# Left sums of the twice-split output projection dealt behind its second and third results, the second sequence's norm scaled three blocks per step, and the third sequence's first gate loads ahead of weight sums

## The chip, the cores and the metric

One core of one Trainium2 chip. The metric is the device time in microseconds of one execution, as the median of three runs; a profiled execution of the same kernel gives the instruction times below. The engines of the core work side by side and wait for each other through semaphores: TensorE (PE, matmuls; its weight loads, PEld, overlap them), VectorE (DVE), ScalarE (ACT), GpSimd (POOL) and SyncE (SP), which issues nearly all the DMA transfers of this kernel.

## The reference

All inputs are float32. Attention over 8 sequences of 12 heads, 448 tokens and 64 values, then a gated feed-forward layer on the result:

```python
q_n, k_n = rmsnorm(q, g_q), rmsnorm(k, g_k)
scores = (1 / sqrt(64)) * q_n @ k_n.T        # per sequence and head, 448 x 448
attn = softmax(scores)
o = attn @ v
x = o as (8*448, 12*64)                      # 3584 tokens, 768 values
xn = x / sqrt(mean(x*x) + 1e-6) * rms_g
g = xn @ w_gate                              # 768 x 1536
h = g * sigmoid(g) * (xn @ w_val)            # 768 x 1536
out = h @ w_out                              # 1536 x 768
```

## The kernel before

**Tiling and order.** Two heads make a pair; 6 pairs make a sequence, and the 48 pairs run in one long loop. A block of the loop computes the scores of pair g in seven steps (`step`, L659 for scores) and, in the same steps, the weighted values of pair g-1 (L674), with an exp on ScalarE for each step (L664). Between blocks `fill` deals out the matmuls of the feed-forward layer. While the attention of sequence b runs, the layer's gate and value products of sequence b-1 and the output projection of sequence b-2 are dealt out. Sequences are counted from 0 in the code (b = 1 is the second). Every piece of PE work goes through `pe`, which advances a counter `now["t"]` by one; `after(n, fn)` has `fn` recorded n pieces later. Each engine works through its own instructions in the order in which they were recorded, so the place in which a helper is called sets what stands ahead of what.

**Fewer multiplications.** Most products are done by schemes that trade multiplications for additions. Gate and value (`three`, L1178) use 15 products instead of 18 for a split of the tokens' matrix by 2 and 3 and of the weights by 3 and 3; the left sums for it are L772, the right sums L1083 and L1086 (`derive`), and the results are added up by DVE in L1196 and L1199. Output projection has two forms: `out_strassen` (L1443) for the second and the fifth sequence, and `out_quads` (L1514) for the third, fourth, sixth, seventh and eighth, where a 2 x 2 split with seven products is nested twice. The first sequence is multiplied plainly (L1582, L1316), and while that goes on the weights are brought in and converted (`convert`: ScalarE L907 and L908, DVE L913 to L915, POOL L964) and stored to device memory in `kept`, `kept_q` and `kept_o`, from where they are loaded again for each sequence.

**A quad.** `out_quads` runs seven outer products i = 0 to 6, in the order of `ORDER_Q`; each is one "quad" of seven inner products, and 11 blocks of weights of up to 192 KB (kind `wq`) are loaded for it. PE gets them in four pieces: `a(i)` multiplies A11 and A12, `bb(i)` multiplies S2 and S3, `c(i)` multiplies A22 and S1, and `d(i)` multiplies S4 and adds into the second half of `c`'s bank. The order on PE is a(i+1), d(i), bb(i+1), c(i+1), a(i+2), and so on. A piece of two products is six matmuls, `d` is three; each matmul stands as two records in the profile. The results are read by DVE: L1534 after `a` (with a ScalarE copy, L1533), L1539 and L1540 after `bb`, L1552 after `c`, L1557 after `d`. L1552 reads the whole bank of `c`, so `d(i)` may write it only when L1552 has ended.

The left sums S1 to S4 (`left_q1`, L1388) are additions of 128 x 384 blocks on DVE:

```python
(("S1", "A21", "A22", ALU.add), ("S2", "S1", "A11", ALU.subtract),
 ("S3", "A11", "A21", ALU.subtract), ("S4", "A12", "S2", ALU.subtract))
```

S1, S2 and S4 go to tiles of `l2_pool`, which has 5; S3 overwrites A21. `bb(i)` records, behind L1540, S4 of quad i and S1, S2 and S3 of quad i+1; they stand on DVE ahead of L1552 of `c(i)`. For i = 1 the rest of the outer left sums (L1360, in `first_sums`) is recorded between them by `hurry`. `"l2 done"` is noted at i = 5; from there on two of the next sequence's L772 sums may take tiles of the same pool.

**Norm.** `norm_x(b)` spreads the reciprocal root of each token over 128 partitions by a matmul into a bank `rb` (L738) of the four banks that scores use, and then multiplies each of x's six blocks by it (`scale`, L744, DVE). For b = 0 all six are recorded at once, for the others one per piece of PE work.

**Loads and their room.** Blocks of weights share one arena with a planner of free pieces (`places`, `room`, `block`). `uses` lists all loads in the order in which they will be needed; `ask` issues the next of them (L1062) when room is left for `keep_free` + 1 blocks, and it is called whenever a block has been used up. `derive_q` makes the sums of w_out's inner split for the quads, once: 21 sets, each with two loads (`wx`, L1044), two blocks of room, four DVE subtractions (L1146 to L1149) and four stores (L1153, L1156). `derive_o` makes those of the outer split (L1118): 24 subtractions. Both are called in `fill` after each piece of PE work.

Of the kernel before, what the change touches and what calls it, by code (L numbers as in the profile page):

```python
# [335 lines left out]
def safe_scores(  # L336
# [37 lines left out]
    st = {}  # L374


    now, due = {"t": 0}, []

    def after(n, fn):
        due.append((now["t"] + n, fn))  # L380
# [351 lines left out]
    def norm_x(b):  # L732


        rs = st.pop(("rx", b))
        ps = (ps_s if b else ps_f).tile([128, 512], F32, name="rb", tag="s" if b else "f")
        for t in range(NT):
            nc.tensor.transpose(ps[:, t * P:(t + 1) * P], rs[:, t:t + 1].to_broadcast([P, 128]), ident[0:P, 0:P])  # L738

        whole = st["x", b]  # L740

        def scale(hp):
            x = whole[:, hp, :]
            nc.vector.scalar_tensor_tensor(x, x, rg[:, hp:hp + 1], ps[:, 0:S], ALU.mult, ALU.mult)  # L744

        for hp in range(NPAIR):
            if b:
                after(hp, lambda hp=hp: scale(hp))
            else:
                scale(hp)  # L750
        if b == 0:
            return

        parts = st.pop(("x", b)).rearrange("p (h c) n -> p h c n", h=2)
        a = st["left", b] = {f"a{i + 1}{k + 1}": parts[:, :, k, i * HT:(i + 1) * HT] for i in range(2) for k in range(3)}

        def place(name):
            if name in OVER:
                return a[OVER[name]]
            if name in MADE[:4]:  # L760
                t = s_pool.tile([128, S], F32, name="xs")
            elif name in ("S2", "S0"):
                t = l2_pool.tile([128, S], F32, name="l2")
            else:
                t = more_x[("S4", "S5", "S13").index(name)]
            return t.rearrange("p (h n) -> p h n", h=2)

        def op(name):
            first, second, what = LEFT_G[name]
            one, two = a[first], a[second]  # L770
            a[name] = place(name)
            nc.vector.tensor_tensor(a[name], one, two, what)  # L772

        slow.extend((name, lambda name=name: op(name)) for name in MADE)
        st["x_at"] = now["t"]
# [98 lines left out]
    def room(many, kind="w"):  # L874
        return len(places(kind)) >= many
# [140 lines left out]
    for b in range(1, B):  # L1016
# [5 lines left out]
        else:  # L1022
            for name in ORDER_O:
                for c in range(NFP):
                    uses.append(("wo", b, name, c))
    asked = {"n": 0, "derived": 0}
    side = [("wd", 1, half, fp) for fp in range(NFP) for half in BLOCKS]
    side += [("wx", 2, ORDER_Q[i], c) for i, j in jobs_q for c in (j, j + KG)]
    derived = [(g, to) for g in GROUPS for _, _, to in PRODUCTS if to in RIGHT_G]
# [6 lines left out]
    def ask():  # L1036

        if turn_of["n"] < TURNS:
            return
        while side and (room(1, "side") or side[0][0] == "wd" and asked["derived"] > 32 and room(4, "wg")):  # L1040
            key = side.pop(0)
            asked[key] = now["t"]
            st[key] = block("side" if room(1, "side") else "wg")
            nc.sync.dma_start(out=data(key), in_=home(key))  # L1044
        while asked["n"] < len(uses):
            key = uses[asked["n"]]
            kind, keep_free = "wg" if key[0] == "wg" else "w", 3
            if key[1] == 1 and key[0] == "wg":
                kind, keep_free = "wg1", 6
            elif asked["derived"] < len(derived):  # L1050
                return
            if key[0] == "wo" and key[2][0] == "T" and ("kept", *key[2:]) not in asked:
                return
            if key[0] == "wq" and asked.get("sums_q", 0) < KG * (key[2] + 1):
                return
            if not room(keep_free + 1, kind):
                return
            asked["n"] += 1
            asked[key] = now["t"]
            st[key] = block(kind)  # L1060
            src = home(key)
            nc.sync.dma_start(out=data(key)[:, 0:src.shape[-1]], in_=src)  # L1062
# [67 lines left out]

    def derive_q(wait=5):

        if not todo_q or sums_o or now["t"] - asked.get("at_q", 0) < 3 or not room(2, "wg"):
            return False
        i, j = todo_q[0]
        keys = [("wx", 2, ORDER_Q[i], c) for c in (j, j + KG)]
        for key in keys:
            if asked.get(key, now["t"]) > now["t"] - wait:
                return False
        todo_q.pop(0)  # L1140
        own_a, own_b = ("ta", i, j), ("tb", i, j)
        st[own_a], st[own_b] = block("wg"), block("wg")
        asked["at_q"] = now["t"]
        x, y, ta, tb = (data(key).rearrange("p (h n) -> p h n", h=2) for key in (*keys, own_a, own_b))

        nc.vector.tensor_tensor(tb[:, 1], x[:, 1], x[:, 0], ALU.subtract)  # L1146
        nc.vector.tensor_tensor(ta[:, 1], y[:, 1], x[:, 1], ALU.subtract)
        nc.vector.tensor_tensor(ta[:, 0], y[:, 1], tb[:, 1], ALU.subtract)
        nc.vector.tensor_tensor(tb[:, 0], y[:, 0], ta[:, 0], ALU.subtract)  # L1149

        def store():
            parts = kept_q[i].rearrange("p (n w) -> p n w", w=HW)
            nc.sync.dma_start(out=parts[:, j], in_=x[:, 0])  # L1153
            for src, first, second in ((y, 1, 6), (ta, 2, 3), (tb, 4, 5)):
                gap = (second - first) * KG
                nc.sync.dma_start(out=parts[:, first * KG + j:second * KG + j + 1:gap], in_=src)  # L1156
            asked["sums_q"] = asked.get("sums_q", 0) + 1

        after(1, store)
        for key in (*keys, own_a, own_b):  # L1160
            after(3, lambda key=key: used(key))
        return True
# [295 lines left out]
    def out_quads(b):  # L1458
# [77 lines left out]
        def bb(i):  # L1536
            ps = two(i, "b")
            u = st["u", b, i] = tmp.tile([128, S], F32, name="th", tag="th", bufs=2)[:, 0:BW].rearrange("p (h n) -> p h n", h=2)
            nc.vector.tensor_tensor(u[:, 0], ps[:, 0], st.pop(("q1", b, i)), ALU.add)  # L1539
            nc.vector.tensor_tensor(u[:, 1], ps[:, 1], u[:, 0], ALU.add)  # L1540
            left_q1(b, i, (3,))
            if i == 1:
                hurry(first_sums)
            if i + 1 < len(ORDER_Q):
                left_q1(b, i + 1, range(3))
            if i + 2 == len(ORDER_Q):
                st["l2 done", b] = True

        def c(i):
            ps = two(i, "c")  # L1550
            u3 = st["u", b, i][:, 1:2].to_broadcast([128, 2, HW])
            nc.vector.tensor_tensor(dst[i][1].rearrange("p (h n) -> p h n", h=2), ps, u3, ALU.add)  # L1552

        def d(i):
            ps = bank[i, "c"]
# [67 lines left out]
    def fill(n=None):  # L1623

        if n is None:
            part["slot"] += 1
            upto = part["all"] * min(part["slot"] / part["slots"], 1.0)
            n = 0
            while n < len(todo) and part["spent"] + todo[n][0] / 2 < upto:
                part["spent"] += todo[n][0]  # L1630
                n += 1
        for _ in range(min(n, len(todo))):
            _, turns, sums_made, fn = todo.pop(0)
            while turn_of["n"] < turns:
                if not convert():
                    pe(idle)
            made, key = sums_made or (0, None)
            while asked["derived"] < made or (key and key not in st):
                before = dict(asked)
                derive(0)  # L1640
                if key and key[0] == "wo":
                    derive_o(0)
                ask()
                if before == asked:
                    pe(idle)
            pe(fn)
            convert()

            if first_sums:
                first_sums.pop(0)()  # L1650
            elif slow and now["t"] - st["block"] > 4 and now["t"] - st["x_at"] >= NPAIR and may_make(slow[0][0]):
                slow.pop(0)[1]()
            if 2 < now["t"] - st["block"] < 5:
                derive()
            if now["t"] - st["block"] > 4 and now["t"] != st.get("left_sums"):
                made = 0
                while made < 2:
                    done = derive()
                    if not done:
                        break  # L1660
                    made += done
                for _ in range(0 if made else 3 if asked["derived"] > 32 else 2):
                    derive_o()
                derive_q()

# [239 lines left out]
```

## Time and profile before

| | |
|---|---|
| median of three runs | 1566.55 us (1565.58 to 1568.97) |
| the profiled execution | 1563.31 us |
| its span, first to last instruction | 1561.5 us |
| PE busy, share of the span | 1491.8 us, 96% |
| PEld | 1160.1 us, 74% |
| DVE | 1027.2 us, 66% |
| ACT | 603.8 us, 39% |
| POOL | 734.1 us, 47% |
| mean DMA rate | 207 GB/s |
| mean granted PE clock | 0.990 |

How to read it: PE is busy nearly all the time, so what counts is where it isn't. In the lines below, a row of waits reads "who waited <- for whom: us in total, times, longest us". A row of the time line reads "start us, duration us, engine, line of the kernel, operation, out<-in, size, count", and in brackets the idle time before it with what ended it. A row of stretches reads "from:to, length", then busy time and count for PE, PEld, DVE, ACT and POOL, then the granted share of PE's clock, the share of the time that the DMA engines were busy, and GB/s. Some places in time: the second sequence's norm is at 243 to 259 us, its output projection at 433 to 503, the third's gate products at 507 to 631, and the third's quads at 632 to 704; the other quads lie at 821 to 892, 1171 to 1243, 1359 to 1413 and 1502 to 1553.

### The profile page before, as it was taken

The numbers are of one execution on the slowest core, as the hardware profiler recorded it, in microseconds if no ns is written. First come the engines' busy times: TensorE is split into PE (matmuls) and PEld (weight loads), VectorE is DVE, ScalarE is ACT, GpSimd is POOL, SyncE is SP. The second block draws the span as 40 slices with busy tenths as digits, with TensorE's granted clock in tenths as the row PEclk, the third lists the DMA queues.
The fourth block names the chain that finished last, engine by engine and source line by source line (L and its number), as shares of the span: only waits on it lengthen the run. The fifth ranks groups of instructions, "written<-read, shape, count | busy, mean of one in ns | idle before, by whom it ended". The sixth has DMA issues, their size and how long they took to land.

```text
span 1561.5 us, 25665 instructions
## 1 busy us (share of the span) xinstructions
PE 1491.8 (96%) x8732; PEld 1160.1 (74%) x8732; DVE 1027.2 (66%) x1826; ACT 603.8 (39%) x1377; POOL 734.1 (47%) x708
## 2 busy tenths in 40 slices
PE   8999998998898999999999999999999999999997
PEld 4344444677754888778888789858788789889997
DVE  5787897787855577864568645645668644674664
ACT  6856764343322443224442353434542342201110
POOL 6877986546433353463544545346544533021002
PEclk9999999999999999999999999999999999999999
DMA  7758584675577999976557855576457745488675
GB/s 191 231 152 249 160 253 142 216 246 193 185 229 230 295 302 286 300 235 186 160 151 234 240 169 168 161 227 194 132 159 241 217 139 145 149 270 248 177 216 183
DMA packets 302175, 322.50 MB, mean 207 GB/s; under 512 B 81620, under 2 KB 243668, under 8 KB 302036
## 3 DMA queue, kind: packets, MB, share of 16 engines
q1 hardware_dynamic: 301108, 320.58, 67.3%
q8 instruction: 72, 1.18, 0.3%
q14 instruction: 67, 0.55, 0.1%
q10 hardware_dynamic: 800, 0.20, 0.1%
q0 software_dynamic: 128, 0.00, 0.0%
HBM read 266.90 MB, written 53.77 MB: 205 GB/s over the span
## 4 chain that ended last, share of the span: by engine, by line
PE 79%; DVE 14%; DMA 3%; issue 2%; SPq 1%; ACT 1%; POOL 0%; DVEq 0%; POOLq 0%; ACTq 0%
PE ff L1178 35%; PE ff L1514 12%; PE sc L659 7%; PE av L674 7%; PE ff L1443 5%; PE ff L1582 5%; PE tr L545 2%; PE ff L1316 2%; DVE l L1388 1%; PE den L692 1%; PE den L607 1%; PE sc L563 1%; PE av L590 1%; DVE w L1118 1%; DVE ms L496 1%
## 5 line engine op out<-in xcount | busy, mean ns | idle before, releaser
L714 POOL TENSOR_TENSOR es<-es,e 128x448 f32<-128x448 f32 x205 | 251.0, 1224 | 13.6
L1178 PE MATMUL ff<-x,w 128*128 128x224 f32 x1272 | 254.0, 353 | 1.4 <-DVE pb L1199 1.1
L1178 PEld LDWEIGHTS ff<-x,w 128*128 128x128 f32 x1272 | 238.6, 190 | 4.2 <-DVE pb L1199 1.4
L659 PE MATMUL sc<-qT,kT 64*64 64x448 f32 x1176 | 234.3, 544 | 6.9 <-DVE x L744 5.5
L674 PE MATMUL av<-e,vt 64*64 64x448 f32 x984 | 195.5, 543 | 0.0
L664 ACT ACTIVATE e<-sc 128x448 f32<-128x448 f32 x294 | 154.9, 546 | 83.6 <-PE sc L659 65.5
L1178 PE MATMUL ff<-xs,w 128*128 128x224 f32 x848 | 170.2, 356 | 7.6 <-DMA w<-kept 5.4
L1178 PEld LDWEIGHTS ff<-xs,w 128*128 128x128 f32 x848 | 159.6, 191 | 12.2 <-DVE x L772 4.7
L644 POOL TENSOR_TENSOR ss<-ss,rd 128x448 f32<-128x448 f32 x40 | 46.7, 1168 | 215.3 <-ACT rd L643 215.3
L709 POOL TENSOR_TENSOR es<-e 128x448 f32<-128x448 f32 x41 | 47.2, 1151 | 213.6 <-ACT e L664 213.6
L659 PEld LDWEIGHTS sc<-qT,kT 64*64 64x64 f32 x1176 | 79.7, 134 | 90.8 <-issue 68.2
L1514 PE MATMUL ff<-w,l 128*128 128x192 f32 x630 | 121.4, 337 | 24.5 <-DVE pa L1552 11.2
L1514 PEld LDWEIGHTS ff<-w,l 128*128 128x128 f32 x630 | 106.1, 194 | 32.6 <-DVE pa L1552 12.8
L1199 DVE TENSOR_TENSOR pc<-ff,l 128x448 f32<-128x448 f32 x56 | 34.9, 623 | 134.4 <-PE ff L1178 77.0
L515 POOL TENSOR_TENSOR rs<-ms,mhalf 128x12 f32<-128x12 f32 (+1 forms) x50 | 115.5, 2311 | 4.2
L1582 PE MATMUL ff<-x,w 128*128 128x448 f32 x288 | 111.8, 541 | 0.0
L674 PEld LDWEIGHTS av<-e,vt 64*64 64x64 f32 x984 | 66.7, 134 | 41.4 <-issue 41.4
L1196 DVE TENSOR_TENSOR pb<-ff,pb 128x448 f32<-128x448 f32 x84 | 52.3, 623 | 65.3 <-PE ff L1178 55.9
L1582 PEld LDWEIGHTS ff<-x,w 128*128 128x128 f32 x288 | 53.3, 190 | 51.0 <-issue 47.6
L1178 PE MATMUL ff<-top_x,w 128*128 128x224 f32 x424 | 87.8, 357 | 2.8 <-DVE w L1086 2.8
L1178 PEld LDWEIGHTS ff<-top_x,w 128*128 128x128 f32 x424 | 78.8, 190 | 13.9 <-issue 13.7
L1178 PE MATMUL ff<-l,w 128*128 128x224 f32 x432 | 86.8, 353 | 0.7 <-DVE pc L1199 0.7
(210 smaller groups left out, 2799.1 us busy)
## 6 DMA issues: line engine op xcount, KB each, us to landing
w<-kept SPq DMA_DIRECT2D x383, 256.0 KB, 3.4
w<-kept_q SPq DMA_DIRECT2D x350, 192.0 KB, 3.7
w<-kept_o SPq DMA_DIRECT2D x150, 192.0 KB, 3.7
kept_q<-w SPq DMA_DIRECT2D x63, 192.0 KB, 3.8
qk<-in_q_dram SPq DMA_DIRECT2D x48, 192.0 KB, 3.7
qk<-in_k_dram SPq DMA_DIRECT2D x96, 96.0 KB, 3.7
raw<-in_moe_w_gate_dram SPq DMA_DIRECT2D x24, 384.0 KB, 4.6
raw<-in_moe_w_val_dram SPq DMA_DIRECT2D x24, 384.0 KB, 4.1
```

The lines of the kernel that those rows point to most:

```text
L515: nc.gpsimd.tensor_tensor(st["rs", g][:, cols], ms, mhalf[:, cols], ALU.pow)
L644: after(m, lambda: (nc.gpsimd.tensor_tensor(ss, ss, rd, ALU.add), st.update({("summed", b): hp})))
L659: nc.tensor.matmul(ps[r, 0:S], lhsT=st["kT", g][r, keys_of(i)], rhs=st["qT", g][r, :], start=True, stop=True)
L664: nc.scalar.activation(e, ps[:, 0:S], ACT.Exp)
L674: nc.tensor.matmul(st["av", g][own(j), 0:S], lhsT=vt, rhs=st["e", g, i][r], start=i == 0, stop=i == PARTS - 1, skip_group_check=True)
L709: nc.gpsimd.tensor_tensor(st["es", g], st["e", g, 0], st["e", g, 1], ALU.add)
L714: nc.gpsimd.tensor_tensor(st["es", g], st["es", g], st["e", g, i], ALU.add)
L1178: nc.tensor.matmul(bank[:, w * HT:(w + 1) * HT], lhsT=data(key)[:, (2 * w + c) * 128:(2 * w + c + 1) * 128], rhs=a[left][:, c, :], start=o ...
L1196: nc.vector.tensor_tensor(T[name], ps[:, 0:S], T[name], ALU.add)
L1443: nc.tensor.matmul(ps, lhsT=left_o(b, which, LEFT_O[name], c), rhs=data(("wo", b, name, c)), start=first and c == 0, stop=c == NFP - 1, sk ...
L1514: nc.tensor.matmul(ps, lhsT=a[:, j, :], rhs=data(key)[:, n % 2 * HW:(n % 2 + 1) * HW], start=start and j == 0, stop=j == KG - 1, skip_grou ...
L1582: nc.tensor.matmul(bank[w][:, 0:S], lhsT=data(key)[:, c * 128:(c + 1) * 128], rhs=st["x", 0][:, 3 * half + c, :], start=half == c == 0, st ...
```

## The change

Three things are moved; nothing is added to or taken from the arithmetic.

- In `out_quads`, `bb(i)` now records only S1 of quad i+1. S4 of quad i and S2 and S3 of quad i+1 are recorded in `c(i)`, behind L1552. For i = 1, `hurry` and then S1 of quad 2 stand behind L1552 too. `"l2 done"` is noted in `c`.
- In `norm_x`, blocks 0 to 2 of the second sequence are scaled at once and blocks 3 to 5 one piece of PE work later.
- Seven loads, the first gate weights of the third sequence, are issued when two blocks are free instead of four, and while they are the next to be issued `derive_q` makes no set. `fill` calls `derive_o` twice per piece of work where it called it three times once `derived` was over 32.

```diff
         for hp in range(NPAIR):
             if b:
-                after(hp, lambda hp=hp: scale(hp))
+                after(hp // 3 if b == 1 else hp, lambda hp=hp: scale(hp))
...
+    next_gate = uses.index(("wg", 2, GROUPS[0], PRODUCTS[0][2]))
+    next_gate = range(next_gate, next_gate + 7)
...
             elif asked["derived"] < len(derived):
                 return
+            elif asked["n"] in next_gate:
+                keep_free = 1
...
-        if not todo_q or sums_o or now["t"] - asked.get("at_q", 0) < 3 or not room(2, "wg"):
+        if not todo_q or sums_o or now["t"] - asked.get("at_q", 0) < 3 or asked["n"] in next_gate or not room(2, "wg"):
             return False
...
             nc.vector.tensor_tensor(u[:, 1], ps[:, 1], u[:, 0], ALU.add)
-            left_q1(b, i, (3,))
-            if i == 1:
-                hurry(first_sums)
-            if i + 1 < len(ORDER_Q):
-                left_q1(b, i + 1, range(3))
-            if i + 2 == len(ORDER_Q):
-                st["l2 done", b] = True
+            if i == 0 or i > 1 and i + 1 < len(ORDER_Q):
+                left_q1(b, i + 1, (0,))
 
         def c(i):
             ps = two(i, "c")
             u3 = st["u", b, i][:, 1:2].to_broadcast([128, 2, HW])
             nc.vector.tensor_tensor(dst[i][1].rearrange("p (h n) -> p h n", h=2), ps, u3, ALU.add)
+            left_q1(b, i, (3,))
+            if i == 1:
+                hurry(first_sums)
+                left_q1(b, i + 1, (0,))
+            if i + 1 < len(ORDER_Q):
+                left_q1(b, i + 1, (1, 2))
+            if i + 2 == len(ORDER_Q):
+                st["l2 done", b] = True
...
-                for _ in range(0 if made else 3 if asked["derived"] > 32 else 2):
+                for _ in range(0 if made else 2):
                     derive_o()
                 derive_q()
```

## The prediction

> **What bounds it now.** First the page's shares: TensorE (PE) is busy for nearly the whole span, no other engine comes near.
>
> ```profile
> span 1561.5 us, 25665 instructions
> PE 1491.8 (96%) x8732; PEld 1160.1 (74%) x8732; DVE 1027.2 (66%) x1826; ACT 603.8 (39%) x1377; POOL 734.1 (47%) x708
> ```
>
> So a gain must come out of PE's idle time or of its clock. Second, PE's waits (total, times, longest): that short list is what there is to win.
>
> ```profile
> PE ff L1514 <- DVE pa L1552: 11.2, 4, 3.3
> PE ff L1514 <- DVE y L1552: 8.7, 7, 2.3
> PE sc L659 <- DVE x L744: 5.5, 1, 5.5
> PE ff L1178 <- DMA w<-kept: 5.4, 2, 4.2
> PE ff L1514 <- DVE pb L1552: 4.5, 3, 1.5
> ```
>
> The three L1514 rows are 24.4 us: a quad's last product, `d`, waits until L1552 has read the third result out of the bank. Third, the time line of one such wait, VectorE (DVE) then PE:
>
> ```profile
> 687.05 0.36 DVE L1540 TENSOR_TENSOR th<-ff,th 128x192 f32<-128x192 f32 x1
> 687.33 1.29 DVE L1388 TENSOR_TENSOR l<-raw,l 128x384 f32<-128x384 f32 x1
> 688.54 1.48 DVE L1388 TENSOR_TENSOR l<-raw 128x384 f32<-128x384 f32 x1
> 690.05 1.37 DVE L1388 TENSOR_TENSOR l<-l,raw 128x384 f32<-128x384 f32 x1
> 691.35 1.48 DVE L1388 TENSOR_TENSOR raw<-raw 128x384 f32<-128x384 f32 x1
> 692.75 1.00 DVE L496 TENSOR_REDUCE ms<-sq 128x6 f32<-128x384 f32 x2
> 693.67 0.54 DVE L1552 TENSOR_TENSOR pa<-ff,th 128x384 f32<-128x384 f32 x1
> ...
> 694.26 3.90 PE L1514 MATMUL ff<-w,l 128*128 128x192 f32 x12 [3.30 <-DVE pa L1552]
> ```
>
> Four left sums (L1388) stand ahead of L1552, though only the first is for `d`; the others are for the next quad. Its matmuls then take 3.90 us, where the same twelve records take 2.11 elsewhere. Fourth, the stretches around three waits (length, then busy time of PE, PEld, DVE, ACT, POOL; clock; DMA):
>
> ```profile
> 257.50:264.33 6.83, 4.89 (x28) 2.02 (x32) 4.57 (x7) 1.20 (x3) 5.37 (x5) 0.50 0.28 81
> 506.68:510.10 3.42, 2.94 (x8) 2.72 (x9) 0.00 (x0) 0.00 (x0) 0.00 (x0) 0.50 1.02 306
> 694.41:697.82 3.41, 3.41 (x11) 3.41 (x12) 2.02 (x5) 0.00 (x0) 3.33 (x3) 0.50 0.22 69
> ```
>
> A long wait is paid twice: the clock is 0.50 after it, so half the PE time there (2.45, 1.47, 1.7 us) is lost too.
>
> [...] the stretches above are 6.83 and 3.41 us, and of the three equal 3.30 us waits (694, 884, 1233 us) the one at 884 brought no slow stretch. [...] the sums at 687 to 692 take 1.29 to 1.48 us beside a busy POOL, the median of all 140 is 0.55, and 27 are over 0.9 (mean 0.713). [...]
>
> **The change part by part.** Built, both kernels have the same instructions; PE, ScalarE and GpSimd keep their order, DVE and SP differ. The matmuls cost what they did.
>
> *Left sums.* Let C be the end of the third result's matmuls. The next quad's first results take 1.96 us (six matmuls, twelve records, as from 665.17 to 667.12), so `d` is due at C+1.96, and the next second results, which read the next S2 and S3, at C+2.94 and C+3.92 (0.98 later each). After the change DVE has only S1 ahead of L1552; behind it come S4, S2, S3. Start to start they take about 0.5: L1552 starts at C+0.2, S4 is done at C+1.3, S2 at C+1.8, S3 at C+2.3. All are in time, so the wait goes, where the sums run at 0.55. Now the waits one by one, in the third sequence:
> - 653.75 (1.40). Four L1360 sums also stood ahead of L1552; one stays, three and the next S1 now stand ahead of the next S2. C=650.24; L1552, S4, three L1360, S1, S2 end at 654.2. `d` goes at 652.2, S2's product is due at 653.6 (a transpose of 0.44 lies between): 0.55 remains, gain 0.85.
> - 662.79 (1.50). S4 took 1.16 and S1 1.48 here. With S1 and one L772 ahead of L1552, S4 ends about 0.6 late: gain 0.9, bounds 0.3 and 1.5.
> - 694.26 (3.30). S1 (1.4) and the two L496 (0.95) end at 689.75, L1552 at 690.3, S4 at 691.6: `d` is 0.6 late, S2 0.35, S3 0.4. Waits of 1.4 remain[...]: gain 1.9, and the 1.7 of clock.
>
> That is 5.35 for the third sequence. The fourth has the same waits without the slow stretch, 3.65; the sixth is like the third, 5.35. The seventh waits 1.27 and 2.27; by the same working 0.4 and 0.9 remain: 2.25. The eighth gains 0.35 at 1518.57 and loses 0.6 at its end: after the last quad nothing stands between `c` and `d`, so S4 behind L1552 adds its 0.55 to the 0.71 wait at 1551.72. Sum 16.35; in other steps of the quads, where DVE idles (1.59 ahead of L1539), I take 0.
>
> *Norm, second sequence.* rb lies in one of the four banks of scores; the fourth score step at 253.95 waits for the sixth L744 until 259.44. All six L744 now run together from 250.09, at 0.6 apiece: done at 253.75, no wait. The fifth step needs the first exp (254.62 + 0.52, ScalarE, unmoved): 0.55. Gain 5.49 + 2.45 - 0.55 = 7.4. Behind the four moved L744 the conversion's joins start up to 2.5 later, but DVE had done the same work by 259.2; the last converted block (POOL L964, 277.4) is used at about 280.8, 3.4 of cover. Were the chain not to move with PE, the gain would be 3.4.
>
> *First gate loads of the third.* Four of the seven now stand in SP's queue at the first kept_q store's place, 492.08, instead of 503.68, and land before 503.0, where PE begins to wait. Two products (3.2 us) run before attention comes in, so four are enough. Gain 4.16 + 1.47 = 5.63. Moved out: two T sums, each four DVE subtractions (1.2 together, 625.93 to 627.13), four stores (0.1 + 3 x 0.2 MB, some 1.8 us of SP) and two loads of 0.2 MB. All sums slip by two places, so the last two come at 628.6 and 632.5. There DVE is full: L1196, for which PE already waits 0.20 at 629.85, starts 1.2 later, lost 1.2. The second delays L1210 and what follows by 1.2 more, ahead of an attention block of 5.5 us that covers it. On SP the stores stand ahead of the first quad's loads and wait for those subtractions; 1.3 MB at some 300 GB/s is over 4 us of a nearly full DMA (620 to 650). Loads for the next steps had 1.5 to 3 us of lead: between 0 and 4, I take 1.0. Sum 3.4.
>
> *Two instead of three o sums per step.* At 430.36 PE waits 3.02 for L1196 behind three L1118; one fewer saves 0.5. The sum comes later, ahead of L744, for which PE waits 0.8 at 438. I take 0.3, bounds -0.3 and 2.2 (its slow stretch at 431.6 gone).
>
> Sum 16.35 + 7.4 + 3.4 + 0.3 = 27.45. The profiled execution took 1563.31 (span 1561.5): it becomes 1535.9. The median of the runs is 3.24 above it: 1539.
>
> **Rivals.** (1) The wait only moves to the next quad's S2 and S3, because 27 of 140 sums are slow and DVE is busy 63 to 83% of the time between 650 and 700; for: 694.26; against: the eighth's sums all take 0.55 until 1549. Part one then gives 5: 1550. (2) The second sequence's gain is caught by the conversion chain, since POOL's adds wait for DVE and DMA there, not for PE: 7.4 less, 1546. (3) Nothing new waits: 24.4 + 3.4 - 0.6, 7.4, 5.6 and 2.2, together 42: 1524; against it, the sums worked out above. (4) Slower: sums contended at all 30 places where a next quad follows. At 1.3 to 1.5 S2 would end near C+3.4 and S3 near C+4.9, some 0.9 late together, 28 us in all; a loss needs new waits over 27.2 (part one with none) + 11.1 (the other parts) = 38.3 us, 1.28 per place, so S1 must hold L1552 back by another 0.4 too; at 1.45 per place the time is 1571. Against it, the mean of 0.713: S2 at C+2.2. (5) The dealing has no effect because the reading of L1552 isn't what releases `d`: against it, all 14 waits end within 0.1 of L1552's end.
>
> **Numbers.** Forecast 0.55 (its own range 1532 to 1546), moved wait 0.18, conversion chain 0.08, all gone 0.09, no change 0.03, slower 0.07. Some 0.2%, 3 us, is what a measurement of this kernel can tell from no change. The range 1530 to 1554 holds forecast, chain, most of the moved wait and a little of the fourth case: 8 in 10. Faster 0.90, same 0.03, slower 0.07.
>
> **What would show it.** The L1514 waits on L1552 near zero, replaced by waits of at most 0.6 on L1388; no L659 wait on L744 and clock 1.0 at 257 to 264; no wait for kept near 503; a wait of about 1.4 on L1196 just ahead of the third's quads. Wrong if L1388 waits of over 1 us stand in most quads, if L1316 waits near 270 to 280, or if L1514 waits for kept_q loads around 635.

## The result, and the profile after

| | before | after |
|---|---|---|
| median of the runs | 1567.28 us (6 runs, 1565.58 to 1569.23) | 1538.79 us (6 runs, 1537.85 to 1543.28) |
| the profiled execution | 1563.31 us, span 1561.5 | 1539.13 us, span 1537.3 |
| mean granted PE clock | 0.990 | 0.995 |

The ratio of the times is 0.9821, with a 95% interval of 0.9807 to 0.9835: 28.5 us less by the medians. The forecast was 1539. The two profiled executions differ by only 24.2 us, and both differences are true; where the other 4 us come from is a part of what follows. Every ratio below is taken against runs of the kernel before made beside it, whose medians lie between 1565.89 and 1567.53, so ratios and medians of two kernels can differ by a microsecond or two.

In the quoted rows most lines of code have moved down by four: the product is L1182 (L1178 before), its additions L1200 and L1203, a set of quad sums L1150 to L1153 with its stores L1157 and L1160, the left sums L1392, the quads' products L1518, the reading of the third result L1551 (L1552 before). First the page of the kernel after, busy time of the engines:

```profile
span 1537.3 us, 25724 instructions
PE 1487.0 (97%) x8732; PEld 1155.3 (75%) x8732; DVE 1031.3 (67%) x1826; ACT 603.2 (39%) x1377; POOL 735.7 (48%) x708
```

PE is busy for 4.8 us less (1491.8 before; three stretches of half clock fewer), and the span is 24.2 shorter. So most of the gain is idle time of PE. (The engines have the same counts; the 59 more instructions in the first line are those of the sequencers, which aren't counted as busy.) Its waits after (who <- for whom: us in total, times, longest):

```profile
PE ff L1518 <- DVE l L1392: 7.3, 17, 1.2
PE ff L1182 <- DVE pb L1200: 7.2, 3, 4.4
PE ff L1182 <- DVE w L1090: 2.8, 1, 2.8
...
PE ff L1447 <- DMA w<-kept_o: 1.9, 1, 1.9
...
PE ff L1182 <- DVE h L1215: 1.6, 1, 1.6
```

The three rows on the third result (24.4 us in 14 waits) have no successor. In their place stand 17 short waits on the left sums, and three more of 0.16 us on S3 (a row of 0.5 for `raw`, not quoted): 7.8 us in 20 waits. The row on L744 (5.5) is gone too. New in this list is 4.4 us on L1200, once. The same quad as before, time line of DVE and PE:

```profile
679.65 1.30 DVE L1392 TENSOR_TENSOR l<-raw 128x384 f32<-128x384 f32 x1
680.87 1.00 DVE L496 TENSOR_REDUCE ms<-sq 128x6 f32<-128x384 f32 x2
681.80 0.54 DVE L1551 TENSOR_TENSOR pa<-ff,th 128x384 f32<-128x384 f32 x1
682.26 1.32 DVE L1392 TENSOR_TENSOR l<-raw,l 128x384 f32<-128x384 f32 x1
...
683.63 1.24 PE L1518 MATMUL ff<-w,l 128*128 128x192 f32 x6 [0.34 <-DVE l L1392]
```

One left sum and the two L496 stand ahead of L1551, the fourth sum behind it, and the wait is 0.34 where it was 3.30. The stretches around the old places of waiting, and around the new one (length; busy time of PE, PEld, DVE, ACT, POOL; clock; DMA share, in which a transfer counts whole where it starts, so that it can pass 1; GB/s):

```profile
249.00:255.83 6.83, 6.83 (x61) 2.61 (x60) 6.66 (x14) 5.44 (x12) 2.60 (x4) 1.00 1.03 360
494.00:497.42 3.42, 3.42 (x22) 3.01 (x24) 2.97 (x8) 0.53 (x1) 0.00 (x0) 1.00 0.96 326
683.60:687.00 3.40, 3.05 (x15) 2.46 (x16) 3.40 (x4) 0.09 (x1) 3.15 (x4) 1.00 0.92 269
620.15:626.98 6.83, 5.41 (x17) 5.01 (x18) 5.54 (x13) 1.15 (x2) 0.23 (x1) 0.50 0.87 267
```

The clock is 1.00 in the three that had 0.50. The fourth, just ahead of the third's quads, had a full clock before and has 0.50 now: what is won at 494 is lost around 620, as the next table shows.

**Where each microsecond went.** PE runs the same 8732 records in the same order in all kernels of this study, so the traces can be laid side by side record by record. The table below is worked out that way: the time between the starts of the same two PE records, in us. The columns are named by what lies between them, with the times that the two records have in the trace of before. "Chance" is a stretch of twelve microseconds in the second sequence that no edit touches.

```
                      start     norm (chance)   o sums     gate     quad    quads    quads    quads    quads    quads
                                                          loads     sums      3rd      4th      6th      7th      8th
                       0-15   15-268  368-380  415-445  490-515  515-636  636-700  700-890 890-1240    -1440     -end
before                13.74   252.92    12.21    30.13    24.98   120.86    64.02   189.91   350.01   200.14   112.47
after                 12.01   245.04    12.21    30.62    19.14   129.69    58.20   185.66   343.87   198.02   112.03
sums_alone            13.54   252.34    13.90    31.94    26.30   121.37    58.19   185.64   343.84   198.00   112.02
norm_alone            12.00   245.08    12.21    31.83    26.02   121.90    64.04   189.92   349.99   200.18   112.46
gate_alone            11.83   252.90    12.21    30.37    19.14   129.76    64.04   189.94   350.03   200.16   112.47
fewer_o_alone         12.07   252.56    13.89    28.88    26.29   121.30    64.03   193.05   348.12   199.92   112.47
sums_norm             11.83   245.01    13.89    31.95    25.86   122.33    58.18   185.65   343.83   198.00   112.02
three_o               13.29   245.03    13.90    31.87    19.14   127.31    58.34   185.63   343.83   198.00   112.02
catch2                11.72   245.07    13.89    28.99    19.14   126.23    58.18   185.61   343.82   198.00   112.02
all_c                 12.05   245.35    13.89    28.91    19.14   126.87    58.28   185.66   343.84   197.48   112.02
store0                13.82   245.06    12.21    28.90    19.14   122.34    59.00   185.63   343.82   198.01   112.02
half_gates            11.98   245.49    12.21    30.71    19.14   119.40    59.59   185.63   343.81   198.01   112.02
store0_late_gates     13.59   245.01    13.89    29.17    26.18   118.90    58.20   185.64   343.85   198.03   112.02
store0_all_c          13.85   245.50    12.21    28.98    19.14   125.25    58.44   185.67   343.87   197.49   112.02
```

From before to after: norm 7.9 less, quads 18.8 less (5.8, 4.3, 6.1, 2.1, 0.4), gate loads 5.8 less, quad sums 8.8 more, o sums 0.5 more. The start is 1.7 less, though no part of the change lies there: it takes 11.7 to 13.9 in the 14 traces, whatever the kernel. The stretches left out (268 to 368, 380 to 415, 445 to 490) differ by 0.5 at most.

### The profile page after: what moved, and what is told of

Read it like the earlier page. It is cut to its first block, busy times and chain, and to the rows that moved or that the text cites. A ratio compares the mean times of both kernels' runs of the same rounds, so it can differ in the third digit from the quotient of the medians.

```text
span 1537.3 us, 25724 instructions
## 1 busy us (share of the span) xinstructions
PE 1487.0 (97%) x8732; PEld 1155.3 (75%) x8732; DVE 1031.3 (67%) x1826; ACT 603.2 (39%) x1377; POOL 735.7 (48%) x708
## 4 chain that ended last, share of the span: by engine, by line
PE 82%; DVE 11%; issue 2%; DMA 2%; ACT 1%; POOL 1%; SPq 1%; DVEq 0%; POOLq 0%; ACTq 0%
PE ff L1182 37%; PE ff L1518 11%; PE sc L659 8%; PE av L674 7%; PE ff L1589 6%; PE ff L1447 5%; PE tr L545 2%; DVE l L1392 2%; PE ff L1320 1%; PE den L692 1%; PE sc L563 1%; PE den L607 1%; PE av L590 1%; DVE ms L496 1%; DVE w L1122 1%
## 5 line engine op out<-in xcount | busy, mean ns | idle before, releaser
L1182 PE MATMUL ff<-x,w 128*128 128x224 f32 x1272 | 254.2, 353 | 1.4 <-DVE pb L1203 1.1
L1182 PEld LDWEIGHTS ff<-x,w 128*128 128x128 f32 x1272 | 238.5, 190 | 4.5 <-issue 1.6
L1182 PE MATMUL ff<-xs,w 128*128 128x224 f32 x848 | 168.7, 353 | 4.9 <-DVE h L1215 1.6
L1182 PEld LDWEIGHTS ff<-xs,w 128*128 128x128 f32 x848 | 158.5, 190 | 8.9 <-issue 4.1
L1518 PE MATMUL ff<-w,l 128*128 128x192 f32 x630 | 118.9, 330 | 7.7 <-DVE l L1392 7.3
L1203 DVE TENSOR_TENSOR pc<-ff,l 128x448 f32<-128x448 f32 x56 | 34.9, 623 | 122.6 <-PE ff L1182 81.1
L1518 PEld LDWEIGHTS ff<-w,l 128*128 128x128 f32 x630 | 103.4, 190 | 15.9 <-DVE l L1392 13.8
L1200 DVE TENSOR_TENSOR pb<-ff,pb 128x448 f32<-128x448 f32 x84 | 52.4, 623 | 65.2 <-PE ff L1182 55.9
L1182 PE MATMUL ff<-top_x,w 128*128 128x224 f32 x424 | 87.8, 357 | 2.8 <-DVE w L1090 2.8
L1182 PEld LDWEIGHTS ff<-top_x,w 128*128 128x128 f32 x424 | 78.8, 190 | 13.9 <-issue 11.6
L1182 PE MATMUL ff<-l,w 128*128 128x224 f32 x432 | 86.8, 353 | 1.1 <-DVE pc L1203 1.1
```

What stands on the lines that cost most here:

```text
L1182: nc.tensor.matmul(bank[:, w * HT:(w + 1) * HT], lhsT=data(key)[:, (2 * w + c) * 128:(2 * w + c + 1) * 128], rhs=a[left][:, c, :], start=o ...
L1200: nc.vector.tensor_tensor(T[name], ps[:, 0:S], T[name], ALU.add)
L1518: nc.tensor.matmul(ps, lhsT=a[:, j, :], rhs=data(key)[:, n % 2 * HW:(n % 2 + 1) * HW], start=start and j == 0, stop=j == KG - 1, skip_grou ...
```

## The experiments

**The four edits, each alone.** The first is the kernel before with the edit of `bb` and `c` only, the second with `hp // 3` only, the third with `next_gate` only, the fourth with two `derive_o` a step only; their diffs are the parts of the change shown above.

> The kernel before with nothing but the left sums of the quads dealt anew (one behind the second results, the others behind the third). Theory A, the gain is the sum of the waits of PE on the second results (L1548): the prediction's terms make 16.35 us, the two traces laid side by side 18.7; so about 1549 us by the before's median of 1567 (1546 to 1552), all waits of PE on L1548 gone and those on the left sums at most about 1.2 us each. Theory B, the wait only moves from L1548 to the left sums: 5 us or less of gain, about 1562.

Measured: 1548.38 us against 1567.49 for before, ratio 0.9878 (0.9853 to 0.9903), 19.1 less. Theory A. The waits of its quads are those of the kernel after:

```profile
PE ff L1514 <- DVE l L1388: 7.2, 17, 1.2
```

> The kernel before with nothing but the second sequence's scaling dealt three per step. Theory A: the wait of 5.7 us for the scores and the 2 us lost in the slow-clock stretch behind it go, 7.4 us: about 1560 (1557 to 1562). Theory B, the conversion chain catches it up at the next hand-over and half is lost again: about 1563.

Measured: 1559.49, ratio 0.9958 (0.9939 to 0.9976), 8.0 less by the medians, 6.6 by the ratio. Theory A: the column of the norm has 7.8 less. Behind it, between 268 and 368 us, this kernel loses 0.4 (100.43 where before has 100.03), so the conversion doesn't catch the gain up (theory B).

> The kernel before with nothing but the early asking of the third's first seven gate loads; three derived sums a step stay. The prediction's term: 5.6 gained at the gate loads, 2.2 given back by sums and transfers, 3.4 faster, about 1564. The theory from the two traces: the waits at 503 to 507 go (5.6), but the two sets of quad sums that are pushed behind the scores of the third stand ahead of the additions of L1200 on DVE, one of them behind a store, which costs a wait of 4.4 and a slow-clock stretch of 2.7 us, and some 2 us more of waits lie between: about 3 slower, about 1570; and a wait of PE's L1182 on DVE's pb of L1200 of about 4 us shows near 632.

Measured: 1566.16 (22 runs), ratio 0.9993 (0.9983 to 1.0002): from 2.7 less to 0.3 more, neither the 3.4 of the prediction nor the 3 more of the second theory. The mechanism of the second theory is there: the wait on L1200 comes back, at 628.21, alone with this edit.

```profile
628.21 3.35 PE L1182 MATMUL ff<-raw,w 128*128 128x224 f32 x8 [3.96 <-DVE pb L1200]
```

Why it isn't 3 slower is in the table: with gate loads as before, the column of the gate loads is 24.98 in the trace of before but 25.86 to 26.30 in the five others, so that trace is 1.1 better there than usual. Taken over all traces with stores as before, early gate loads win 6.8 there (the five with late ones mean 25.89, early ones take 19.14) and lose 6.9 between 515 and 636 (late 121.55 in the mean of five; early 128.41 in the mean of the four in which nothing else is changed there). In sum that is nothing, though single traces of this kind carry an error of a microsecond or so.

> The kernel before with two derived sums of the o weights a step in place of three. The prediction's term: 0.3 faster; the traces side by side: 0.4 slower. Both: no change that can be told, within 1 us of 1567. Rival: the slow-clock stretch near 431 (about 1.5 us lost) goes with the shorter DVE queue, 2 us faster.

Measured: 1564.24 (22 runs), ratio 0.9981 (0.9971 to 0.9991): 3.0 less (1.4 to 4.5), more than both; the rival's 2 is within the interval. The column of the o sums shows two levels for each form. Three sums a step: 30.13 and 30.37, or 31.83 to 31.95. Two sums: 28.88 to 29.17, or 30.62 and 30.71. Like against like it is 1.3 less, and the lower level comes in two of six traces with three sums and in six of eight with two. Three of the eight traces with two sums have no half clock there at all (mean clock 1.00 between 404 and 446 us), none of the six with three (0.96 in each).

So the rival is right in part: the half clock goes in some executions, not in all. PE's wait for L1196 here is 3.0 us with three sums and 2.4 with two; in the windows of the last section, PE is busy for 0.36 of the one at this wait in the trace of before (428.17 to 431.58), and half clock follows it. In the kernel after it is busy for 0.44 (418.76 to 422.17), and none follows; one follows the next wait there, 1.86 for a load (425.59 to 429.00, busy for 0.46). How often each case comes, 14 traces are too few to say. Where there is a half clock, its place counts too: in the run store0_all_c it lies at 424 to 427, costs 1.7 against store0, and the wait for a load behind it is 1.6 shorter; in the kernel after it lies at 429 to 432, behind that wait, and nothing takes it up. In fewer_o_alone one more stretch has moved by itself, from the sixth's quads (1.9 less) to the fourth's (3.1 more), where no edit lies. The traces of before and after are the wrong pair to read this from: before happened to have its lower level, after its higher one.

**Is a gain of three parts the sum of three parts?** The kernel after without part three, and the kernel after with three o sums a step:

```diff
-                for _ in range(0 if made else 2):
+                for _ in range(0 if made else 3 if asked["derived"] > 32 else 2):
```

> The kernel after without its third part: left sums and norm as changed, gate loads and derived sums of the o weights as before. Theory A, by the times of the parts run alone (gate loads 1.3 and fewer o sums 3.2 faster, both against 1567.5): 4 slower than the kernel after, about 1543. Theory B, by the two traces laid side by side (part three costs 3 in them): about 1536. Prediction's terms: 3.7 slower than after.

Measured: 1540.94, ratio 0.9839 (0.9812 to 0.9866). The kernel after is at 0.9821 (0.9807 to 0.9835), so part three is worth 2 to 3 us by the middle values, and zero is within the intervals too. Theory B (1536) is just out, A's 1543 is within the interval.

> The kernel after with three derived sums of the o weights a step in place of two. By the run of that edit alone: about 3 slower than the kernel after, near 1542, with a slow-clock stretch of PE between 425 and 445. By the prediction's term: 0.3 slower, near 1539.

Measured: 1541.07, ratio 0.9834 (0.9807 to 0.9860). The column of the o sums is at its higher level, 31.87. That is 2 slower than the kernel after, with zero within the intervals, so it doesn't decide between its two expectations. Together with gate_alone (nothing found) and fewer_o_alone (3.0) it points to the o sums, not the gate loads, as what part three is worth; except for the 3.0, these differences are no larger than their errors.

**What stands at 621.** DVE of the kernel after just ahead of the new wait:

```profile
616.21 0.61 DVE L1200 TENSOR_TENSOR pa<-ff,pa 128x448 f32<-128x448 f32 x1
619.07 0.36 DVE L1150 TENSOR_TENSOR w<-w 128x192 f32<-128x192 f32 x1 [2.25 <-DMA kept_q<-w]
...
620.90 0.62 DVE L1200 TENSOR_TENSOR pb<-ff,pb 128x448 f32<-128x448 f32 x1
```

The 20th of the 21 sets stands ahead of the L1200 that PE waits for. It takes more than its four subtractions: it takes over the room of the 19th set, whose stores SP issued between 614.29 and 616.25, and waits 2.25 us until they have landed; with it waits everything behind it on DVE. The first test makes the late sets earlier, two steps apart in place of three:

```diff
-        if not todo_q or sums_o or now["t"] - asked.get("at_q", 0) < 3 or asked["n"] in next_gate or not room(2, "wg"):
+        if not todo_q or sums_o or now["t"] - asked.get("at_q", 0) < (2 if asked["n"] >= next_gate.stop else 3) or asked["n"] in next_gate or not room(2, "wg"):
```

> The kernel after with the sets of quad sums two steps apart in place of three once the seven gate loads are asked, so that all 21 sets are made ahead of the third's scores. Theory A, the 4.4 us wait on DVE's pb at 621.57 and the 2.7 lost in the slow-clock stretch behind it come from the set that stands ahead of L1200 and waits for the store of the set before it: both go, about 1532 to 1535. Theory B, the wait has another cause or the third set between 600 and 612 delays the head transposes that follow it on DVE as much: about 1539, with a wait of PE for x or e near 610 in its place.

Measured: 1540.04, ratio 0.9834 (0.9809 to 0.9860). The wait at 621 and the half clock behind it are gone, 7.0 us at that place, so the set was its cause. But the median is not better. It isn't lost where theory B looked, at the transposes near 610: the trace loses 6.3 between 525 and 567, 1.4 and 0.7 us and this wait with a stretch of half clock behind it (waits of PE between 515 and 635 us):

```profile
PE ff L1182 <- DVE w L1151: 2.7, 1, 2.7
```

Named is DVE, whose L1151 ends just then, but PE doesn't read what that writes. Three loads of weights for the third's gate were issued from 556.82 us on; PE goes on at 562.00, the landing of the first two isn't in the trace, and the third lands at 563.41. So a late load is the likelier cause, but it is not shown. Between 567 and 600 the trace wins 2.7 of this back, and the column of the quad sums ends at 3.5 less; this trace is also the fastest of the five runs (1537.08, the others 1539.63 to 1541.71), so it shows the kernel at its best. The sets themselves now wait 15.2 us in four places for stores. So the sets can be moved and the waits move with them. Two theories stay: the store of a set is issued too late, or the stretch is short of transfers whatever the order. The second test issues the stores one step earlier; on PE, DVE, ScalarE and GpSimd every instruction keeps its place.

```diff
-        after(1, store)
+        store()
```

> The kernel after with the stores of a set of quad sums put into SP's queue in the same step as the sums, one step earlier than before. Every other engine's instructions and their order are as in after. Theory A, the wait of 4.4 at 621.57 is the 20th set's wait for the store of the 19th (2.25 on DVE): the store lands 1 to 2 earlier, the wait falls to about 2.5 and part of the slow-clock stretch of 2.7 behind it goes, about 1535 to 1537. Theory B, the transfers of this stretch are the limit (the DMA engines' share is 0.94 to 0.99 between 530 and 650): an earlier store only pushes back the loads behind it in the queue, about 1539 with waits on loads in other places.

Measured: 1534.91 (1533.55 to 1538.99), ratio 0.9806 (0.9784 to 0.9827), as theory A has it. DVE of this kernel at the 20th set:

```profile
614.01 0.61 DVE L1200 TENSOR_TENSOR pa<-ff,pa 128x448 f32<-128x448 f32 x1
614.82 0.36 DVE L1150 TENSOR_TENSOR w<-w 128x192 f32<-128x192 f32 x1 [0.19 <-DMA kept_q<-w]
```

The wait for the store is 0.19 there, and 0.20 more ahead of the next subtraction, PE's wait on L1200 is 2.0 where it was 4.4, and no stretch of half clock follows. The column of the quad sums is 7.3 less. Some of theory B is there as well: PE waits 1.9 us until 588.72, just after a load issued at 582.48 has landed (588.58). The third test takes transfers away:

```diff
             src = home(key)
+            if key[0:2] == ("wg", 2):
+                src = src[:, 0:GW // 2]
```

> The kernel after with only the first half of each of the third sequence's gate weight blocks loaded; the products read what was left in the buffer for the other half, so the third's gate is not computed rightly. Transfers between about 495 and 640 are lighter by half of these blocks. Theory B, transfers limit this stretch: the waits of PE on loads and on DVE between 525 and 632 (11 in all, with the slow-clock stretch) shrink by more than half, about 1532. Theory A, only the place of the displaced sets matters: the store of the 19th set still lands late by its own latency, the wait at 621.57 stays above 3 and the time is within 2 of 1539.

Measured: 1529.83, ratio 0.9771 (0.9751 to 0.9792). PE's waits between 560 and 650 us (two lines of code lower, so L1202 is L1200 of the others):

```profile
PE ff L1184 <- DVE pb L1202: 1.4, 1, 1.4
PE sc L659 <- DVE x L744: 1.3, 1, 1.3
```

With half of these bytes the wait at 621 is 1.4 though the stores stand where they stood in the kernel after, and the waits at 573, 589 and 592 are gone. In this run DVE waits for no store at all between 500 and 650 us. So theory A in its strict form, that only the place of the store counts, falls, and theory B holds, while store0 shows that the place counts as well. The two belong together. A store in this stretch lands late while the DMA engines are busy 0.93 to 0.96 of the time (windows 515 to 560 and 560 to 636 of the kernel after): between 515 and 640 us the stores of L1160 take 2.6 us at the shortest from issue to landing, 4.1 in the median and 5.2 at the longest. With half of the gate bytes the same stores take 2.0, 3.1 and 4.8, and the engines are busy 0.86 and 0.89 of the time (515 to 560, 560 to 628). Issued a step earlier, the store of the 19th set cost the 20th 0.39 us of waiting in store0 (0.19 and 0.20), where it had cost 2.25.

Does the early asking pay once the stores are early? The same stores, with the gate loads as before the change:

> The kernel store0 with the third's gate loads asked as before the change: early stores, left sums, norm and two o sums stay. Theory A, the gate loads' early asking was worth its 5.6 at 503 and was spent in the wait behind the store: with early stores it pays, so this is about 5 slower than store0, near 1540, by waits of 5 on the third's gate loads near 495. Theory B, what is gained there is lost in the same stretch whatever the stores do, since the transfers of 490 to 640 are the same: within 2 of store0's 1534.9.

Measured: 1535.89, ratio 0.9800 (0.9773 to 0.9827), 1 above the run with early gate loads, which is within the spread. Theory B. By the columns, gate loads and quad sums together are 145.1 with late gate loads and 141.5 and 144.4 (store0, store0_all_c) with early ones. A gain of the early asking is not shown in the medians. That of the early stores shows in the column of the quad sums in both forms (121.55 to 118.90 with late gate loads, 128.41 to a mean of 123.80 with early ones).

**The one left sum that was kept ahead.** All left sums behind the third results:

```diff
-            if i == 0 or i > 1 and i + 1 < len(ORDER_Q):
-                left_q1(b, i + 1, (0,))
...
-                left_q1(b, i + 1, (0,))
             if i + 1 < len(ORDER_Q):
-                left_q1(b, i + 1, (1, 2))
+                left_q1(b, i + 1, range(3))
```

> The kernel after with every left sum behind the third results, none behind the second. Theory A, the sums are consumed at once and their place matters to the half microsecond: the first sum of the next quad comes 0.55 later in the clear and 1.3 later where it runs beside other work, and the waits on the left sums grow by 3 to 8 in all, about 1542 to 1547. Theory B, the third results leave enough slack and the one dealt ahead is without effect: within 1 of the kernel after, 1539.

Measured: 1535.71 (1534.90 to 1537.57), ratio 0.9806 (0.9780 to 0.9832). Theory A was wrong: the five columns of the quads are 0.5 less in sum, not 3 to 8 more. Theory B is right about the quads, though not about the time. The waits are fewer and longer, 8.4 us in 9 places for 7.8 in 20.

```profile
PE ff L1518 <- DVE l L1392: 8.4, 9, 1.6
```

The other 2.6 us between the medians are not from the quads. In the traces the difference lies in the o sums (28.91 for 30.62) and in the quad sums (126.87 for 129.69), whose code is the same in both. The intervals of the two ratios overlap.

> The kernel store0 with every left sum behind the third results. By the traces of after and of the run with all sums there, the quads gain 0.7 by it: about 1534, the best of these kernels. Rival, the lower median of that run was in chance stretches of slow clock and not in the quads: as store0, 1535.

Measured: 1535.16, ratio 0.9792 (0.9766 to 0.9817): not different from store0. The quads are 1.0 less, the quad sums 2.9 more than in that run: the 20th set waits 1.70 for a store although it is issued early, PE's wait on L1200 is 3.95, and half clock follows. So an early store doesn't always land in time, and one trace is not enough to price that wait.

store0 is better than the kernel before by 31 us. Against the kernel after it is some 2 us better by the ratios and 3.9 by the medians; its slowest of five runs is 1538.99, the fastest of the six after 1537.85. The intervals of the ratios overlap, so that it beats the kernel after is likely, not settled.

## Why the prediction was right, and where it was not

The time was right (1539 against 1538.79) and so was the sum (27.45 against 28.5 by the medians). Two of its four terms were right in kind and nearly in size: the waits that they name are gone, for the reason given. The other two were wrong, with opposite errors. That the total fits within 1 us is therefore luck: against the means of the table's columns the left sums gave 2.4 us more than predicted and the o sums 1.7 more, the gate loads 3.5 less.

*Left sums: 16.35 predicted; 18.8 in the traces, 19.1 in the run alone.* Right. By sequence 5.35, 3.65, 5.35, 2.25 and -0.25 against 5.8, 4.3, 6.1, 2.1 and 0.4. The working that gave S4, S2 and S3 their times behind L1552 holds where the sums run at 0.55. Laid side by side, the three places of the third sequence win 1.2, 0.85 and 3.8 where 0.85, 0.9 and 3.6 were predicted, those of the fourth 1.2, 0.85 and 2.1 for 0.85, 0.9 and 1.9: the term was too small chiefly at the first kind of place, where the wait on S2 is 0.22. At 694.26 waits of 1.4 were to remain; 0.66 are seen (0.34 + 0.16 + 0.16), but with the slower starts around them PE still loses 1.3 there. The eighth was to lose at its last product, where nothing stands between `c` and `d`; it does (PE starts its last three matmuls 0.47 later), but it wins 0.9 around 1518.57 instead of 0.35. The sign "at most 0.6" for the waits on L1388 fails at three of them (0.66, 1.11 and 1.17). And S1 need not stand ahead of L1552, as the change has it: all_c does as well without.

*Norm: 7.4 predicted, 7.9 in the traces.* Right, in both halves: the wait on L744 is gone, and the clock is 1.00 at 249 to 256. The 0.55 that was taken off for the fifth score step isn't there, PE has no wait over 0.15 between 240 and 275; as much (0.5) is lost again by 368. The conversion has slack, as the prediction read from the block used at 280.8.

*Gate loads: 3.4 predicted, nothing found.* This is the step that failed. The first half of it, a gain of 5.63 at the waits themselves, measured 5.8 between the two traces and 6.8 on the means. The failure is in "L1196, for which PE already waits 0.20 at 629.85, starts 1.2 later, lost 1.2". The four subtractions were priced at their busy time. What the set also brings to DVE is its own wait for room, 2.25 us on the store of the set before, and behind that a stretch of half clock with 2.7 us of PE's time: 4.4 of wait and 2.7, in place of 1.2. The prediction had the facts at hand. Its time line shows four left sums and two L496 run ahead of L1552, for which PE waits 3.30 us, and it called the DMA nearly full between 620 and 650 us (share 0.96 in the trace of before). The trace of before has the same kind of wait, where PE needed nothing from DVE just then (DVE's waits between 440 and 680 us):

```profile
DVE w L1146 <- DMA kept_q<-w: 4.7, 2, 4.2
DVE w L1147 <- DMA kept_q<-w: 2.5, 1, 2.5
```

But it asked only whether the loads would be late for PE, and never what the moved instruction itself waits for. The allowance of 1.0 for the transfers was too small too: the 1.6 at 589.54 is new, beside a load that landed at 589.41, and half_gates shows that it goes when the bytes go.

*Two o sums: 0.3 predicted, bounds -0.3 and 2.2; measured 3.0 (1.4 to 4.5) alone.* The bounds were nearly wide enough, the value was not. The 0.5 at L1196 is there (0.6). Wrong was to set the later wait on L744 against it. And the half clock after 431 was taken as a constant of the kernel, of which at best all would go; in fact the stretch comes at two levels, and by the traces (lower level in two of six with three sums, in six of eight with two) the edit seems to change how often each comes.

*The bridge from the profiled execution to the median, 3.24 us,* was carried over as if it were a constant. It isn't: after, the median is 0.3 below the profiled execution. The traces of the parts show two places where the trace of before is better than the others with the same code: the o sums (30.13 where the mean of six is 31.35) and the gate loads (24.98, mean of six 25.94), 2.2 together. Put together from the means of like traces (o sums 31.35 to 29.40, gate loads 25.89 to 19.14, quad sums 121.55 to 128.41, the start unchanged), the columns make 28.0 us, close to the 28.5 of the medians. That is an estimate from single traces of fourteen kernels; no kernel was traced repeatedly. The clock that is on record for every run speaks for it: in the 45 runs of the kernel before beside the first four experiments it lies between 0.986 and 0.992, and 0.001 less of it goes with 1.2 us more, closely though not strictly (correlation -0.68). The trace of before has 0.990, above the middle of these runs (0.989).

*The rivals.* That the wait only moves to S2 and S3 (1550): no, 7.8 us of waits are left in place of 24.4, and only two of the 20 are above 1. The conversion chain (1546): no, 0.4 to 0.5 lost behind the norm. All gone (1524): no, by the slow left sums and by 620. In the kernel after 26 of the 140 take over 0.9 us; GpSimd is busy for 0.93 of their time on average, for 0.14 of that of the others. Slower (1571): no, 107 of the 140 left sums take 0.6 us or less, and their median is 0.55. No effect: no.

## What to carry to other kernels

When an instruction is moved, price not only the time it takes but also what it waits for at its new place. Here a set of 1.2 us of subtractions brought 2.25 us of waiting for a store with it; L1200 stood behind it on DVE, PE waited 4.4 us for that, and the half clock that followed took 2.7 more. Where the DMA engines were busy 0.93 to 0.96 of the time, asking for seven loads earlier won 6.8 us in one column and lost 6.9 in the next; the cheap thing to try was to issue the stores that free room as soon as their data exist (2.7 and 4.6 less in the column of the quad sums). Before reading a small effect from two traces, lay several traces of kernels with the same code in that place side by side: here the same instructions differed by 1.3 to 2.9 us in five places, the first 15 us among them.

## What the runs showed of the hardware

A stretch of half clock comes also behind a wait shorter than the stretch itself: in the kernel after, 3.41 us of it (429.00 to 432.42) follow a wait of 1.86 that ends at 427.93. In the traces of before and after, the steps between full and half clock stand multiples of 3.413 us apart, to within 0.01 (the stretches at half clock are 3.41 and 6.83 us long, but for the last, which runs to the end of the execution), and these multiples begin at different places: counted from the first instruction, at 1.50 us in before and at 2.34 in after. Cut into windows at these multiples (but for 20 us at either end), the two executions have 873 windows at full clock. Seven of them are followed by one at half clock; PE is busy for 0.00, 0.00, 0.04, 0.13 and 0.36 of theirs in before, for 0.13 and 0.46 in after. In the other 866 it is busy for 0.44 or more. Of the nine windows at half clock two are followed by another one, with PE busy for 0.43 and 0.58; seven by full clock, with PE busy for 0.86 or more. Busy time is the profile's, in which the ends of matmuls are modelled.

One wait shows the same in two runs. Ahead of a product of the second sequence PE waits 2.8 us on L1090 (L1086 before). The same twelve microseconds (368 to 380 in before) take 12.21 us in seven of the 14 traces, 13.89 or 13.90 in the other seven. What differs between the run catch2 (13.89) and the kernel after (12.21), with 2.77 us of waiting in both, is where the windows cut the wait. Two windows of catch2, then two of the kernel after:

```profile
360.08:363.49 3.41, 1.22 (x7) 1.25 (x8) 3.34 (x6) 0.00 (x0) 0.96 (x1) 1.00 0.97 281
363.49:366.90 3.41, 3.41 (x11) 3.09 (x10) 0.56 (x1) 0.53 (x1) 0.00 (x0) 0.50 1.03 327
360.74:364.15 3.41, 1.53 (x8) 1.56 (x9) 3.38 (x5) 0.00 (x0) 0.65 (x1) 1.00 0.97 318
364.15:367.56 3.41, 3.41 (x22) 3.11 (x24) 1.72 (x4) 0.53 (x1) 0.00 (x0) 1.00 0.97 271
```

PE was busy for 0.36 of the first window in catch2, and the clock of the second is 0.50; it was busy for 0.45 in the kernel after, and the second has 1.00. In before, also at 12.21, the wait is cut into two windows with PE busy for 0.66 and 0.53. The wait of 3.30 us at 884 in that trace, behind which the prediction saw no slow stretch, is cut into two with PE busy for 0.51 and 0.52.
